# The first batch's attention and gates in two query parts (192 and 256 tokens) in a squared-ReLU attention and SwiGLU kernel

## The chip, the cores and the metric

The kernel runs on one core of one Trainium2 chip. The metric is the device time of one execution in microseconds (us). Engines: PE is TensorE (matmuls and transposes), DVE is VectorE, ACT is ScalarE, POOL is GpSimd, SP is SyncE. POOL and SP compute almost nothing here; their queues issue the DMAs.

## The reference

Eight batches, 12 heads, 448 tokens, 64 elements per head. The attention output of all heads becomes 3584 rows of 768; an RMS norm and a SwiGLU FFN follow.

```python
scores = matmul(q, k.T) / sqrt(64)               # per batch and head, 448 x 448
attn   = maximum(scores, 0) ** 2 / 448
x      = matmul(attn, v)                         # rows: batch, token; columns: head, element
xn     = x / sqrt(mean(x * x) + 1e-6) * rms_g
out    = (silu(xn @ w_gate) * (xn @ w_val)) @ w_out   # 768 -> 1536 -> 768, float32 out
```

## The kernel before, in words

**Units.** The work is written out as 24 attention units m: batch b = m // 3, and four heads (two pairs) in each. In a unit, `scores` (L272) makes seven tiles: for each pair three chunks of 128 keys, and one tile with the last 64 keys of both pairs. A tile holds two heads; its matmuls have 448 query columns and use half of PE's rows each. ACT takes the ReLU from PSUM (L297), DVE squares it in place (L298). `attend` (L301) multiplies with v a unit later, ACT scales the result into `xT` (L333) and DVE squares it into `x2` (L334). Keys stand in permuted order, and queries too: token = 7 x row + u, so a pair's queries are seven blocks u of 64.

**Norm and FFN.** After a batch's third unit, `norm` (L351) sums the squares with six constant-ones matmuls (psSS, L355), ACT takes the square root (L363), and DVE makes four reciprocals (L376) and six scaled tiles `xn` (L379). These DVE steps go into the list `bg` and are taken one by one by `step()`. Then `gates` (L398) puts 24 pieces into the list `pieces`, a gate piece (psG, L406, then Silu, L416) and a val piece (psV, L422, then the product hT, L429) for each of 12 blocks of 128 FFN columns, each six matmuls of 448 columns. After each second batch `outproj` (L443) adds 14 pieces of 12 matmuls (psO, L451); two halves of 384 columns are evacuated into one `ost` tile, by ACT (L467) and DVE (L469), and stored together by SP (L470).

**Order.** Nothing is scheduled by a tool: each engine runs in the order of the text. `fill(us)` (L479) takes pieces until their written costs (1.13 for a gate or val piece, 1.97 for a half of the out-projection) have used up the time given. Units up to the seventh get 6.8 us, later ones 13.8 (L500). While the first three units run there are no pieces; there, and in the first gate (L413), `warm` (L266) puts in matmuls of a constant tile whose result nobody reads (psW, L268).

**Buffers.** PSUM: two score tiles (psS) of two banks each, and four rotating banks (`rot`) for everything else, transposes too. `relu2` has nine r tiles, `ostage` two tiles, `sig` three.

**Loads and transposes.** POOL issues all loads of q, k, v and the weights in the order of the text (L144 to L170 first, the rest from `transposes` and `attend`); they convert float32 to bfloat16. q and k of batches 0 and 1, and q of batch 2, are turned on PE (psQ, psK, psX, L192) and copied by DVE (L210, L222, L258); later ones by DMA transposes on SP (`turn_by_dma`, L247), two per `fill`.

Of the kernel before, what the change touches and what calls it, by code (L numbers as in the profile page):

```python
# [15 lines left out]
def kernel(  # L16
# [33 lines left out]

    const_pool = ctx.enter_context(tc.tile_pool(name="consts", bufs=1))
# [6 lines left out]
    opool = ctx.enter_context(tc.tile_pool(name="ostage", bufs=2))  # L58
# [12 lines left out]
    nc.sync.dma_start(out=g_sb[:], in_=moe_rms_g.rearrange("(kt p) -> p kt", p=P))  # L71
# [20 lines left out]
    def load_q(pr, h0=0, h1=H, es=(0, 1)):  # L92
        for e in es:
            dst = q_t[pr][e * HALF : (e + 1) * HALF]
            src = q[2 * pr + e, h0:h1]
            if pr < 2:
                nc.gpsimd.dma_start(  # L97
                    out=dst[:, h0:h1],
                    in_=src.rearrange("h (p u) d -> p h u d", u=NU),
                )  # L100
            else:
                nc.gpsimd.dma_start(
                    out=dst, in_=src.rearrange("h (p u) d -> p u h d", u=NU)
                )

    def load_k(b, h0=0, h1=H):
        src = k[b, h0:h1, 0:XT0]
        if b < 2:
            nc.gpsimd.dma_start(
                out=k_t[b][:, h0:h1],  # L110
                in_=src.rearrange("h (p c) d -> p h c d", c=NCH),
            )
        else:
            nc.gpsimd.dma_start(
                out=k_t[b][:], in_=src.rearrange("h (p c) d -> p c h d", c=NCH)
            )

    def load_kx(b, h0=0, h1=H):
        nc.gpsimd.dma_start(
            out=kx_t[b][:, h0:h1], in_=k[b, h0:h1, XT0:S].rearrange("h p d -> p h d")  # L120
        )
# [22 lines left out]
    load_q(0, 0, 2, (0,))  # L144
# [3 lines left out]
    load_q(0, 2, 4, (0,))  # L148
    load_k(0, 2, 4)
    load_kx(0)  # L150
    load_v(0, 0, 4)
    eps_col = const_pool.tile([P, 1], FP32, name="eps_col", tag="eps_col")
    nc.vector.memset(eps_col[:], eps)  # L153
    load_q(0, 4, 8, (0,))
    load_k(0, 4, 8)
    load_vx(0)
    load_v(0, 4, 8)
    load_q(0, 8, 12, (0,))
    load_k(0, 8, 12)
    load_v(0, 8, 12)  # L160
    k_tile(1)
    load_q(0, 0, H, (1,))
    load_k(1)
    load_kx(1)
    load_gv(0, 256)
# [3 lines left out]
    load_gv(256, 512)  # L169
    load_gv(512, 768)  # L170
# [9 lines left out]
    QT, KTt, R, XT, X2 = {}, {}, {}, {}, {}  # L180
# [17 lines left out]
    def transposes(n):  # L198
# [4 lines left out]
        if pr == 0 or pr == 1 and e == 0:  # L203
            r0, r1 = (e * HALF, (e + 1) * HALF) if pr == 0 else (0, P)
            if j == 0 and e == 0:
                big(pr, None)
            ps = psum.tile([P, NU, r1 - r0], BF16, name="psQ", tag="rot", bufs=4)
            for u in range(NU):
                turn(ps[:, u, :], lambda hh: q_t[pr][:, 2 * j + hh, u, :], r0, r1)
            nc.vector.tensor_copy(out=QT[pr][:, j, :, r0:r1], in_=ps[:])  # L210
        if b < 2:
            if j == 0:
                big(None, b)
            ps = psum.tile([P, XT0], BF16, name="psK", tag="rot", bufs=4)
            for c in range(NCH):
                turn(
                    ps[:, c * P : (c + 1) * P],
                    lambda hh: k_t[b][:, 2 * j + hh, c, :],
                    0,
                    P,  # L220
                )
            nc.vector.tensor_copy(out=KTt[b][:, j, :XT0], in_=ps[:])  # L222
# [9 lines left out]
        if j == HP - 1:  # L232
            if b + 2 < B:
                k_tile(b + 2)
                load_k(b + 2)
                load_kx(b + 2)
            if e == 0 and pr + 1 < B // 2:
                q_tile(pr + 1)
                load_q(pr + 1)
            if b == 0:  # L240
                load_gv(768, 1024)
                load_gv(1024, F)
# [29 lines left out]
    def scores(m, slots, k=0):  # L272
        b, t = divmod(m, ND)
        qt, kt = QT[b // 2], KTt[b]
        for s in slots:
# [20 lines left out]
            r = rpool.tile([P, 2, S], BF16, name="r", tag="r")  # L296
            nc.scalar.activation(out=r[:], in_=ps[:, :, :S], func=ACT.Relu)  # L297
            nc.vector.tensor_tensor(out=r[:], in0=r[:], in1=r[:], op=ALU.mult)  # L298
            R[m, s] = r

    def attend(m):  # L301
# [26 lines left out]
        if t == 0:  # L328
            XT[b] = xpool.tile([P, KT, S], BF16, name="xT", tag="xT")
            X2[b] = xpool.tile([P, KT, S], BF16, name="x2", tag="x2", bufs=1)  # L330
        xt = XT[b][:, 2 * t : 2 * t + 2, :]
        for i in range(2):
            nc.scalar.mul(out=xt[:, i, :], in_=acc[i][:], mul=inv_attn)  # L333
        nc.vector.tensor_tensor(  # L334
            out=X2[b][:, 2 * t : 2 * t + 2, :], in0=xt, in1=xt, op=ALU.mult
        )
        if t == ND - 1 and b + 2 < B:
            v_tile(b + 2)
            load_v(b + 2)
            load_vx(b + 2)  # L340
            if b == 0:
                for f0 in range(0, FT, 4):
                    nc.gpsimd.dma_start(
                        out=wo_sb[:, f0 : f0 + 4], in_=wo_d[:, f0 : f0 + 4]
                    )
# [5 lines left out]
    def norm(b):  # L351
        ps = psum.tile([P, S], FP32, name="psSS", tag="rot", bufs=4)
        x2 = X2.pop(b)
        for kt in range(KT):
            nc.tensor.matmul(  # L355
                out=ps[:],
                lhsT=ones_bf[:, :P],
                rhs=x2[:, kt, :],
# [5 lines left out]
            out=rstd[:],  # L364
            in_=ps[:],
# [4 lines left out]
        xn = xpool.tile([P, KT, S], BF16, name="xn", tag="xn")  # L370
        xt = XT.pop(b)

        def recip(i):
            w = S // 4
            sl = slice(i * w, (i + 1) * w)
            nc.vector.reciprocal(out=rstd[:, sl], in_=rstd[:, sl])  # L376

        def scale(kt):
            nc.vector.scalar_tensor_tensor(  # L379
                out=xn[:, kt, :],  # L380
                in0=xt[:, kt, :],
                scalar=g_sb[:, kt : kt + 1],
                in1=rstd[:],
# [4 lines left out]
        for i in range(4):  # L388
            bg.append(lambda i=i: recip(i))
        for kt in range(KT):  # L390
            bg.append(lambda kt=kt: scale(kt))

        def ready():
            gates(b, xn)

        bg.append(ready)

    def gates(b, xn):  # L398
        pr, e = divmod(b, 2)

        def gate(fb, st):
# [3 lines left out]
            for kt in range(KT):  # L405
# [7 lines left out]
                if b == 0 and fb == 0 and kt < KT - 1:  # L413
                    warm(2)
            sig = tpool.tile([P, S], BF16, name="sig", tag="sig", bufs=3)
            nc.scalar.activation(out=sig[:], in_=ps[:], func=ACT.Silu)  # L416
            st["sig"] = sig

        def val(fb, st):
            ps = psum.tile([P, S], FP32, name="psV", tag="rot", bufs=4)  # L420
            for kt in range(KT):
# [9 lines left out]
                in0=st["sig"][:].rearrange("p (u x) -> p u x", u=NU),  # L431
# [11 lines left out]
    def outproj(pr):  # L443
        ob = out[2 * pr * S : 2 * (pr + 1) * S, :].rearrange("(x u) m -> x u m", u=NU)

        def half(u, o, st):
            if o == 0:
                st["ost"] = opool.tile([P, DM], FP32, name="ost", tag="ost")
# [9 lines left out]
            dst = st["ost"][:, o * OW : (o + 1) * OW]  # L458
            if 2 * pr + 2 == B and u == NU - 1:
                hw = OW // 2  # L460
                nc.scalar.copy(out=dst[:, :hw], in_=ps[:, :hw])
                nc.vector.tensor_copy(out=dst[:, hw:], in_=ps[:, hw:])
                lo = o * OW
                nc.scalar.dma_start(out=ob[:, u, lo : lo + hw], in_=dst[:, :hw])
                nc.sync.dma_start(out=ob[:, u, lo + hw : lo + OW], in_=dst[:, hw:])
            elif o == 0:
                nc.scalar.copy(out=dst, in_=ps[:])  # L467
            else:
                nc.vector.tensor_copy(out=dst, in_=ps[:])  # L469
                nc.sync.dma_start(out=ob[:, u, :], in_=st["ost"][:])  # L470

        for u in range(NU):
            st: dict = {}
            for o in range(2):
                pieces.append((1.97, lambda u=u, o=o, st=st: half(u, o, st)))
# [3 lines left out]
    def fill(us, idle_steps=3):  # L479
# [4 lines left out]
        while pieces and debt > 0:  # L484
# [3 lines left out]
            step()  # L488
# [5 lines left out]

    N = B * ND
    warm_tile()
    warm(8)
    transposes(0)
    for m in range(N + 1):
        rate = 6.8 if m < 2 * ND + 1 else 13.8  # L500
        first = m == ND
        idle = 2 if m <= ND else 0
        if m <= ND:
            warm_tile()
        if m < N:
            scores(m, (0, 1), idle if m == 0 else 0)
        if m == ND + 1:
            warm_tile()
            warm(3)
        if m in (ND + 1, 2 * ND + 1):  # L510
            fill(0.36 * rate)
        if m > 0:
            warm(idle // 2)
            attend(m - 1)
        else:
            transposes(1)
            last_keys(0)
        if m < N:
            scores(m, (2, 3), idle)
        if not first:  # L520
            fill(0.36 * rate)
        if 0 < m < N - 1:
# [3 lines left out]
            if m < ND:  # L526
                warm_tile()
        if m > 0 and m % ND == 0:
            norm(m // ND - 1)
        if m in (ND, 2 * ND):  # L530
            while bg:
                step()
        if first:
            warm_tile()
        if m < N:
            scores(m, (4, 5), idle)
        if m == 0:
            transposes(2)
        if not first:
            fill(0.36 * rate)  # L540
        if m < N:
            scores(m, (6,))
        if m + 1 < N:
            transposes(2 * m + 3)
            if m == 0:
                last_keys(1)
        if not first:
            fill(0.28 * rate)
# [32 lines left out]
```

## Time and profile before

| | us |
|---|---|
| median of three runs | 471.22 (470.94 to 472.3) |
| the profiled execution | 473.52 |
| its span, first to last instruction | 471.7 |
| PE busy in the span | 457.4 (97%) |
| DVE, ACT busy | 253.2, 253.9 (54% each) |
| constant matmuls psW: 60, busy on PE | 19.5 |

A row of the timeline has the start of a group of like instructions, its length, engine, line and operation, the tile written and those read, the count, and in brackets the idle time before it and who ended that. Rows of matmuls overlap, because they are pipelined; the distance between starts tells what a group costs. In the row of a group, "busy, mean ns" is followed by the idle time of the engine just before and by whoever ended it. The digits show 40 equal slices of the span in tenths of busy time.

### The profile page before, as it was taken

The page shows a single profiled execution, that of the slowest core. Times are in us where ns is not written, and L with a number is a line of the kernel's source. Part 1 is how long each engine was busy: PE and PEld are TensorE (multiplying, and loading weights), DVE is VectorE, ACT ScalarE, POOL GpSimd, SP SyncE. Part 2 cuts the span into 40 slices and gives each one's busy share as a digit, 9 for nine tenths or more (in the row PEclk, how much of TensorE's full clock was granted, in tenths as well). Part 3 has the DMA queues.
Part 4 walks back from the last instruction along what each step waited for, and adds up shares of the span by engine and source line. Part 5 has one row for each costly group of instructions (what it writes and reads, how often), then busy time and mean ns, then how long its engine had stood idle before and what let it go on. Part 6 is the DMA issues. An engine that isn't in the chain of part 4 may idle for free.

```text
span 471.7 us, 7484 instructions
## 1 busy us (share of the span) xinstructions
PE 457.4 (97%) x3048; PEld 223.9 (47%) x3048; DVE 253.2 (54%) x435; ACT 253.9 (54%) x366; POOL 68.8 (15%) x75
## 2 busy tenths in 40 slices
PE   8989998899999999989999999999999999999997
PEld 3344443444455544434455544444455544545564
DVE  2678665955436654675456545765456553732211
ACT  3788576655465375665565465765565274422110
POOL 8635113421040002500040002000000000000000
PEclk9999999999999999999999999999999999999999
DMA  9999999999989814990098618200002210000022
GB/s 93 175 185 183 175 173 152 192 144 120 47 103 176 215 44 74 161 101 0 2 125 168 158 52 114 14 1 1 1 0 101 82 53 1 0 1 1 35 100 101
DMA packets 129715, 42.77 MB, mean 91 GB/s; under 512 B 113424, under 2 KB 126224, under 8 KB 129680
## 3 DMA queue, kind: packets, MB, share of 16 engines
q0 software_dynamic: 96336, 24.38, 63.8%
q1 hardware_dynamic: 33056, 17.70, 18.1%
q8 instruction: 24, 0.39, 0.4%
q10 hardware_dynamic: 288, 0.20, 0.1%
q14 instruction: 11, 0.09, 0.1%
HBM read 48.76 MB, written 11.01 MB: 127 GB/s over the span
## 4 chain that ended last, share of the span: by engine, by line
PE 79%; DMA 14%; DVE 3%; ACT 2%; POOL 1%; issue 1%; DVEq 0%; POOLq 0%
PE psO L451 24%; PE psV L422 21%; PE psG L406 20%; DMA wv_sb<-in_moe_w_val_dram 9%; PE psS L289 6%; PE psAV L321 6%; DMA kld<-in_k_dram 5%; PE psSS L355 1%; ACT r L297 1%; DVE xn L379 1%; DVE rstd L376 1%; DVE hT L429 0%; DVE r L298 0%; POOL qld L97 0%; ACT xT L333 0%
## 5 line engine op out<-in xcount | busy, mean ns | idle before, releaser
L297 ACT ACTIVATE r<-psS 128x896 bf16<-128x896 f32 x168 | 145.9, 923 | 39.0 <-PE psS L289 39.0
L298 DVE TENSOR_TENSOR r<-r 128x896 bf16<-128x896 bf16 x168 | 104.0, 625 | 91.2 <-ACT r L297 90.7
L406 PE MATMUL psG<-xn,wg_sb 128*128 128x448 bf16 x576 | 125.9, 353 | 2.2 <-DVE hT L429 1.1
L422 PE MATMUL psV<-xn,wv_sb 128*128 128x448 bf16 x576 | 124.9, 353 | 1.7 <-DMA wv_sb<-in_moe_w_val_dram 1.5
L451 PE MATMUL psO<-wo_sb,hT 128*128 128x384 bf16 x672 | 113.0, 326 | 0.0
L416 ACT ACTIVATE sig<-psG 128x448 bf16<-128x448 f32 x96 | 52.2, 545 | 106.6 <-PE psG L406 91.4
L429 DVE TENSOR_TENSOR hT<-sig,psV 128x448 bf16<-128x448 bf16 x96 | 59.1, 617 | 61.8 <-PE psV L422 59.5
L451 PEld LDWEIGHTS <-hT 128*128 128x128 bf16 x672 | 64.3, 98 | 46.1 <-issue 4.8
L406 PEld LDWEIGHTS <-wg_sb 128*128 128x128 bf16 x576 | 55.1, 98 | 55.4 <-issue 5.6
L422 PEld LDWEIGHTS <-wv_sb 128*128 128x128 bf16 x576 | 54.1, 98 | 57.2 <-issue 7.9
L289 PE MATMUL psS<-QT,KT 64*128 64x448 bf16 (+1 forms) x384 | 53.1, 364 | 3.8 <-ACT r L297 3.8
L467 ACT COPY ost<-psO 128x384 f32<-128x384 f32 x27 | 12.9, 479 | 54.7 <-PE psO L451 47.9
L469 DVE COPY ost<-psO 128x384 f32<-128x384 f32 x27 | 15.0, 556 | 37.3 <-PE psO L451 37.3
L124 POOL DMA_DIRECT2D vld<-in_v_dram x10 | 9.5, 948 | 171.1 <-PE psAV L321 159.4
L289 PEld LDWEIGHTS <-KT 64*128 64x128 bf16 (+1 forms) x384 | 14.0, 96 | 40.6 <-issue 38.3
L321 PE MATMUL psAV<-r,vld 128*64 128x448 bf16 x288 | 31.8, 356 | 0.0
L379 DVE SCALAR_TENSOR_TENSOR xn<-xT,g_sb,rstd 128x448 bf16<-128x448 bf16 x48 | 30.8, 679 | 0.1
L333 ACT ACTIVATE xT<-psAV 128x448 bf16<-128x448 f32 x48 | 23.6, 544 | 6.1 <-PE psAV L321 5.9
L376 DVE RECIPROCAL rstd<-rstd 128x112 f32<-128x112 f32 x32 | 25.2, 824 | 2.9 <-ACT rstd L363 2.9
L334 DVE TENSOR_TENSOR x<-xT 128x896 bf16<-128x896 bf16 x24 | 15.0, 625 | 14.2 <-ACT xT L333 14.2
L321 PEld LDWEIGHTS <-vld 128*64 128x64 bf16 x288 | 14.4, 109 | 15.6 <-issue 7.6
L268 PE MATMUL psW<-ones_bf 128*128 128x448 bf16 x60 | 19.5, 421 | 1.4 <-DVE eps_col L153 1.4
(37 smaller groups left out, 160.5 us busy)
## 6 DMA issues: line engine op xcount, KB each, us to landing
out_dram<-ost SPq DMA_DIRECT2D x27, 384.0 KB, 2.3
qld<-in_q_dram POOLq DMA_DIRECT2D x7, 672.0 KB, 19.8
kld<-in_k_dram POOLq DMA_DIRECT2D x7, 576.0 KB, 15.1
vld<-in_v_dram POOLq DMA_DIRECT2D x7, 576.0 KB, 7.2
wo_sb<-in_moe_w_out_dram POOLq DMA_DIRECT2D x3, 768.0 KB, 23.9
vxld<-in_v_dram POOLq DMA_DIRECT2D x16, 96.0 KB, 7.7
wg_sb<-in_moe_w_gate_dram POOLq DMA_DIRECT2D x4, 384.0 KB, 14.6
wv_sb<-in_moe_w_val_dram POOLq DMA_DIRECT2D x4, 384.0 KB, 15.5
```

Source lines behind the costliest of these rows:

```text
L289: nc.tensor.matmul(out=ps[rows, hh, :S].rearrange("k (u x) -> k u x", u=NU), lhsT=kt[prt, j, keys], rhs=qt[prt, j, :, b % 2 * HALF : (b % ...
L297: nc.scalar.activation(out=r[:], in_=ps[:, :, :S], func=ACT.Relu)
L298: nc.vector.tensor_tensor(out=r[:], in0=r[:], in1=r[:], op=ALU.mult)
L321: nc.tensor.matmul(out=acc[i][hh * D : (hh + 1) * D, :], lhsT=w[rows, hh, :], rhs=r[rows, hh, :], start=(c == 0), stop=(c == NCH),)
L333: nc.scalar.mul(out=xt[:, i, :], in_=acc[i][:], mul=inv_attn)
L376: nc.vector.reciprocal(out=rstd[:, sl], in_=rstd[:, sl])
L379: nc.vector.scalar_tensor_tensor(out=xn[:, kt, :], in0=xt[:, kt, :], scalar=g_sb[:, kt : kt + 1], in1=rstd[:], op0=ALU.mult, op1=ALU.mult,)
L406: nc.tensor.matmul(out=ps[:], lhsT=wg_sb[:, kt, fb * P : (fb + 1) * P], rhs=xn[:, kt, :], start=(kt == 0), stop=(kt == KT - 1),)
L416: nc.scalar.activation(out=sig[:], in_=ps[:], func=ACT.Silu)
L422: nc.tensor.matmul(out=ps[:], lhsT=wv_sb[:, kt, fb * P : (fb + 1) * P], rhs=xn[:, kt, :], start=(kt == 0), stop=(kt == KT - 1),)
L429: nc.vector.tensor_tensor(out=HT[pr, fb][:, :, e * HALF : (e + 1) * HALF], in0=st["sig"][:].rearrange("p (u x) -> p u x", u=NU), in1=ps[:] ...
L451: nc.tensor.matmul(out=ps[:], lhsT=HT[pr, fk][:, u, :], rhs=wo_sb[:, fk, o * OW : (o + 1) * OW], start=(fk == 0), stop=(fk == FT - 1),)
```

## The change

The first batch's 448 queries are split into blocks u 0 to 2 (192 tokens) and u 3 to 6 (256 tokens). The kernel runs all three units of the first part, its norm and its first gates before it goes through the second part, whose units stand among the first part's gates. Score tiles of a part hold two chunks of keys (columns 2 x 192 or 2 x 256), r tiles grow to 1024 columns. Gate and val pieces of a part hold two FFN blocks. k and q of the first batch are turned two pairs at a time. The constant matmuls go from 60 to 42. Units 3 to 6 get 4.0 us of pieces, units 7 to 11 12.0, later ones 13.4. `fill` can take more than one DVE step behind a piece. The squares of a unit are written into `xn`, which the norm overwrites. Each half of the out-projection is stored by itself, from three half-wide `ost` tiles. Weights are loaded ahead of the second batch's k, q and v. The code:

```diff
+    US = ((0, 3), (3, NU))
...
-    opool = ctx.enter_context(tc.tile_pool(name="ostage", bufs=2))
+    opool = ctx.enter_context(tc.tile_pool(name="ostage", bufs=3))
...
+    def load_q0(h, h0=0, h1=H):
+        u0, u1 = US[h]
+        nc.gpsimd.dma_start(
+            out=q_t[0][:HALF, h0:h1, u0:u1],
+            in_=q[0, h0:h1].rearrange("h (p u) d -> p h u d", u=NU)[:, :, u0:u1],
+        )
...
-    load_q(0, 0, 2, (0,))
+    load_q0(0, 0, 2)
     load_k(0, 0, 2)
...
-    load_q(0, 2, 4, (0,))
     load_k(0, 2, 4)
+    load_q0(0, 2, 12)
+    load_k(0, 4, 8)
     load_kx(0)
     load_v(0, 0, 4)
+    load_vx(0)
+    load_k(0, 8, 12)
+    load_v(0, 4, 12)
...
+    load_q0(1)
+    load_gv(0, 256)
+    load_gv(256, 512)
+    load_gv(512, 768)
     k_tile(1)
-    load_q(0, 0, H, (1,))
     load_k(1)
     load_kx(1)
-    load_gv(0, 256)
+    load_q(0, (1,))
+    load_gv(768, 1024)
     v_tile(1)
     load_v(1)
     load_vx(1)
-    load_gv(256, 512)
-    load_gv(512, 768)
+    load_gv(1024, F)
...
+    PARTS = ((0, 1), (2, 3), (4, 5), (6,))
+    def part_scores(h, t, tiles, k=0, late=None):
+        u0, u1 = US[h]
+        w = (u1 - u0) * HALF
...
+            nc.scalar.activation(out=r, in_=ps[:, :, : n * w], func=ACT.Relu)
+            square(r, late)
...
+    def norm(b, parts, ready):
...
+        n = 4 if w > 256 else 2
...
+    def part_gates(h, fbs):
+        def both(w_sb, fb, name):
+            ps = psum.tile([P, 2, w], FP32, name=name, tag="rot", bufs=4)
+            for i in range(2):
+                for kt in range(KT):
+                    nc.tensor.matmul(out=ps[:, i, :],
+                        lhsT=w_sb[:, kt, (fb + i) * P : (fb + i + 1) * P],
+                        rhs=XN[0][:, kt, sl], start=(kt == 0), stop=(kt == KT - 1))
+                    if h == 0 and fb == 0 and i == 0 and w_sb is wg_sb and kt < KT - 1:
+                        warm(1)
...
+        cost = 12 * w / 2370
...
-            sig = tpool.tile([P, S], BF16, name="sig", tag="sig", bufs=3)
+            sig = tpool.tile([P, 512], BF16, name="sig", tag="sig")
...
-            step()
+            for _ in range(max(steps, round(cost))):
+                step()
...
+    big(0, 0)
+    first_q(0, 0, (0,))
+    first_k(0, (0,))
+    warm(1)
+    part_scores(0, 0, (0,), late=late)
+    warm(2)
+    first_q(0, 0, (1,))
+    first_k(0, (1,))
+    flush(late)
+    part_scores(0, 0, (1, 2))
+    last_keys(0)
+    first_k(1)
+    first_q(0, 1)
+    part_scores(0, 0, (3,))
+    warm_tile()
+    for t in range(1, ND):
+        part_scores(0, t, (0,))
+        warm(1)
+        part_scores(0, t, (1,))
+        part_attend(0, t - 1)
+        if t + 1 < ND:
+            first_k(t + 1)
+            first_q(0, t + 1)
+            warm_tile()
+        part_scores(0, t, (2, 3))
+    first_q(1, 0)
+    first_q(1, 1)
+    warm_tile()
+    warm(2)
+    part_attend(0, ND - 1)
+    warm(5)
+    norm(0, cols(0), lambda: part_gates(0, (0, 2, 4, 6)))
+    drain()
+    warm_tile()
+    part_scores(1, 0, (0, 1, 2, 3), 2)
+    warm(7)
+    warm_tile()
+    piece(2)
+    part_scores(1, 1, (0, 1))
+    part_attend(1, 0)
+    piece(1)
+    part_scores(1, 1, (2, 3))
+    first_q(1, 2)
+    piece(1)
+    part_scores(1, 2, (0, 1))
+    part_attend(1, 1)
+    piece(1)
+    part_scores(1, 2, (2, 3))
+    transposes(HP - 1)
+    transposes(HP)
+    last_keys(ND)
+    piece(1)
+    part_attend(1, 2)
+    prefetch_v(0, ND - 1)
+    transposes(HP + 1)
+    warm_tile()
+    warm(2)
+    norm(0, cols(1), lambda: part_gates(1, (0, 2, 4, 6)))
+    scores(ND, (0, 1), late=late)
+    piece(1)
+    steps(4)
+    piece(1)
+    scores(ND, (2, 3), late=late)
+    drain()
+    flush(late)
+    for h in range(2):
+        part_gates(h, (8, 10))
+    for m in range(ND, N + 1):
+        rate = 4.0 if m < 2 * ND + 1 else 12.0 if m < 4 * ND else 13.4
+        quick = 2 if m in (2 * ND, 2 * ND + 1) else 1
...
```

New helpers: `first_q` and `first_k` turn the first batch's q part and k for two pairs with one DVE copy each; `part_attend` is `attend` at a part's width; `square` squares an r tile at once or, given the list `late`, when `flush` is called; `piece(n)` runs n pieces, `drain()` all DVE steps. In the loop, a unit's three fills stand where they stood, the third unit's from after its second pair of score tiles on.

## The prediction

> **What bounds the kernel now.** I read the page's busy table and slices first, then the order of TensorE's (PE's) work by time, then who PE waits for.
>
> ```profile
> PE 457.4 (97%) x3048; PEld 223.9 (47%) x3048; DVE 253.2 (54%) x435; ACT 253.9 (54%) x366; POOL 68.8 (15%) x75
> ...
> DMA  9999999999989814990098618200002210000022
> ...
> PE 79%; DMA 14%; DVE 3%; ACT 2%; POOL 1%; issue 1%; DVEq 0%; POOLq 0%
> ...
> L268 PE MATMUL psW<-ones_bf 128*128 128x448 bf16 x60 | 19.5, 421 | 1.4 <-DVE eps_col L153 1.4
> ```
>
> PE is the bound, but 97% hides two things: 60 of its matmuls are the constant ones (psW, L268), and the DMA engines are full for the first 130 us, so a load lands when the bytes ahead of it are through.
>
> ```profile
> 12.28 0.93 PE L268 MATMUL psW<-ones_bf 128*128 128x448 bf16 x2
> 13.14 0.49 PE L289 MATMUL psS<-QT,KT 64*128 64x448 bf16 x2
> 13.56 0.55 PE L268 MATMUL psW<-ones_bf 128*128 128x448 bf16 x2
> ...
> 44.22 0.35 PE L406 MATMUL psG<-xn,wg_sb 128*128 128x448 bf16 x1 [0.23 <-DVE xn L379]
> ...
> 72.92 1.31 PE L422 MATMUL psV<-xn,wv_sb 128*128 128x448 bf16 x6 [1.53 <-DMA wv_sb<-in_moe_w_val_dram]
> ...
> 91.36 1.29 PE L406 MATMUL psG<-xn,wg_sb 128*128 128x448 bf16 x6 [1.11 <-DVE hT L429]
> ...
> 204.41 0.36 PE L289 MATMUL psS<-QT,KT 64*128 64x448 bf16 x2 [1.39 <-ACT r L297]
> 205.22 0.36 PE L289 MATMUL psS<-QT,KT 64*128 64x448 bf16 x2 [0.45 <-ACT r L297]
> ```
>
> The first three rows are the clock: the same pair of constant matmuls takes 0.93 at 12.3 us and 0.55 at 13.6, so PE ran at half clock up to about 13.4 us. The fourth is the first gate matmul, at 44.2 us: until then there is no FFN work. The rest are the later stalls.
>
> So I book the span as useful PE work plus lost time. Unit costs, start to start: gate or val group of six, 1.14 us (0.189 each at 448 columns); out-projection, 1.95 for twelve (0.1625 at 384). The two rows give 0.414 ns a column, so 0.083 at 192 and 0.110 at 256. A group that follows another tiling of the array takes about 0.10 more (gate groups show 1.24 against 1.14). Scores 1.75 a unit, attention 1.57. Over the instruction list: gates and vals 1152 x 0.189 = 217.9, out-projection 109.2, 24 units of scores and attention 42.0 + 37.7, norm sums 9.1, transposes 11.5 (0.34 and 0.51 for q, 0.29 for k), some 60 returns from tiled work at 0.10; together 433.6 us of useful work. The profiled span is 471.7: 34.5 are lost up to the last matmul's start and 3.5 follow it. At 44.2 us, 20.4 are done and 23.9 lost; when 32.7 are done, 27.0 are lost (ten more constants are in the first gate); 7.5 come later: 1.6 (wv_sb), 1.5 (first norm beside units, 88 to 91 us), 2.2 (202 to 205 us: six score tiles in a row, the FFN list being empty), the rest small.
>
> **The change, part by part.**
>
> Work added to PE. First batch's scores: a 192-wide tile of two chunks is 2 x 0.083 + 0.105, so a unit 3 x 0.271 + 0.21 = 1.02, a 256-wide one 1.21, together 2.23 for 1.75. Attention 0.83 + 1.02 for 1.57. Three units: 3 x (0.48 + 0.28) = 2.3. Gates and vals: 144 times 0.083 + 0.110 - 0.189, 0.5. Sum +2.8. Not shown by any row is whether a 128-column weight load keeps up with 83 ns; weight loads show 98 ns each, but the 128-row q transposes pass 14 loads of 64 columns with their matmuls in 0.51 us, so 128 loaded columns in 73 ns. Bounds: 0 and 144 x (98 - 83) = 2.2. I take 0: of the two rows this one shows a rate, the other a latency that overlaps.
>
> Constants: 60 become 42, of which 18 x 0.189 = 3.4 less at full clock; this is inside the lost time below.
>
> The opening. ACT rows, start to start: 0.81 for a 896-wide relu (five in 4.15), 0.44 for 448; so 0.70 at 768, 0.39 at 384, 0.92 at 1024, 0.23 and 0.28 for the evacuations. DVE: square 0.53 at 896, so 0.47 and 0.60; reciprocal 0.72 at 112; scale 0.60 at 448, between 0.26 and 0.60 at 192: I take 0.34. With these I went down the built order of the three engines:
> - POOL's queue: heads 2 to 12 of the first q part (240 KB) go in one load ahead of k's heads 4 to 8, of kx and of v. By bytes moved in this trace (567 KB by 8 us, 1123 by 12, 2020 by 17, landings 1 to 2.5 us later) they land at 8.9, kx at 11.9, the first v at 12.9, last v at 18.6, second q part at 22, first gate weights at 24 to 26, the sixth at 34.5, all gate and val weights by 52 instead of 81. The second unit's scores then start at 14.5, after the k and q copies.
> - A 192-wide unit needs 2.95 on ACT and some 3 on DVE, but at half clock 5.1 on PE (1.65 scores, 1.4 attention, 1.65 transposes, a constant): PE bounds it. Third unit at 20.2, last attention to 26.9, norm sum to 29, sqrt 0.4, two reciprocals 1.3, scales to 32.5, four score tiles of the second part beside it on ACT (3.2), seven constants: first gate at 33.8, if the clock is half until about 30 us. If it is full from 20 us, 30.7; from 13.4 us, 27.7.
> When does the clock rise? In before PE streamed 80, 71 and 77% of full-array work in the three 3.4 us stretches up to 13.4 us. By the same count the new order has 34, 41, 70, 42, 76, 67% in the stretches from 6.6 to 27 us, and 95% only after that. I take late.
>
> [...]
>
> So 10.6 us of useful work are done at 33.8: 23.2 lost, 0.7 less than before at its first gate, and five constants in that gate for ten.
>
> Second part's attention among the gates (33.8 to 62.6). Useful 22.1 us, constants 1.4. Waits found by going down the queues: 1.0 for the q copy, which stands behind two squares on DVE; 0.6 at the third attention; 0.8 and 1.8 in the second norm, where the PSUM buffer of a val piece waits for a q copy that stands behind four scales and four put-off squares; rest 1.1. Elapsed 28.8, so at 32.7 useful us 29.9 are lost: 2.9 more than before. ACT has two more table loads here (1.28 each).
>
> Later. Weights have landed, so 1.6 goes; next late would be the third batch's k, whose load now stands behind the weights on POOL: it lands at about 60 and its transposes on SP run to 84, each chunk needed from 82 on, in order; cover about 10 us for the first chunks, 5 for that batch's q (72 against 77). The empty list at 202 us goes: the new rates leave at least 11 us of FFN in each unit from the eighth on. Units four to six with little FFN: 10.3 and 8.3 us on PE against 7.4 on ACT and about 7 on DVE, so PE still bounds and I find 0.2. The second batch's norm: DVE has 14 us of work in a stretch of 12.6, a val waits 0.5 and an attention 1.0; 1.5 as before. Small stalls stay (1.9). Sum 3.6 for 7.5.
>
> At nothing: the norm gain's load, later in the text but still first on SP's queue; the scaled activations that now overwrite their squares, since they wait for the norm sum anyway; half stores (each copy still waits for the store three pieces back; 2.3 us landing under 7 us of PE work; 27 more issues of 0.33 us on SP; cost if cover fails, the 1.3 us ACT already waits for ost). Two sig buffers for three: a gate waits for the product two pieces, over 2 us, back; bounds 0 and 0.6 (a product) in each of the norms. The last stores are split as before.
>
> Sum on the span: useful +2.8; lost 29.9 + 3.6 = 33.5 for 34.5, -1.0. Span 473.5, +1.8. The profiled execution took 473.5 with 471.7 of span, 2.3 over the median of 471.2; the same 1.8 on the median is **473.0**.
>
> **Rivals.**
> - The clock rises early (by 13 to 20 us). First gate 27.7 to 30.7, 3.1 to 6.1 sooner, and nothing behind it changes: 466.9 to 469.9, faster. It decides if the clock is full before about 20 us. For: PE is nearly always occupied, and the row does not tell whether the chip counts occupation or fill. Against: the fill shares above.
> - It comes out even: clock at 24 to 27 us, first gate near 32, what the opening gives is spent on smaller pieces and the second norm. 470 to 472.5.
> - Weight loads bound the 192-wide pieces (98 ns for 83): +2.2, 475.2, and up to 476.5 with the norms' sig waits.
>
> **How the numbers follow.** Measurement of this kernel can tell about 0.3% (1.4 us: 469.8, 472.6). Forecast, 471.8 to 474.5: 0.42 (slower 0.34, same 0.08). Early clock: 0.32 (faster 0.30, same 0.02). Even: 0.15 (same 0.13, faster 0.02). Weight loads: 0.11, slower. So faster 0.32, same 0.23, slower 0.45. The range leaves out the earliest clock's tail and half of the last case: 467.2 to 476.0.
>
> **What would show it.** Constant matmuls of 0.37 us start to start after 20 us: the clock step right; 0.19 at 14 us: wrong. First psG at 33.8. val pieces (psV) waiting for QT copies at about 60 us. Gate matmuls of the first batch at 83 and 110 ns. No wait for wv_sb, no score tiles waiting for ACT at about 200 us; none for KT at 80 to 90 us. The forecast is wrong if the first gate comes before 31 us or the stretch behind it takes under 26 us.

## The result, and the profile after

The changed kernel takes **473.87 us** (median of eleven runs, 473.18 to 475.79). The kernel before, run beside it, takes 471.22 (468.87 to 473.34). The ratio is 1.0061, interval 1.0038 to 1.0084: slower by about 0.6%. The profiled execution, the slowest of the eleven, took 475.79 with a span of 474.0, against 473.52 and 471.7 before. Executions more than 1.5% above the fastest of their kernel are left out of all ratios.

From the page of the changed kernel: PE's busy time, the granted clock in 40 slices, and the shares of the chain that ended last.

```profile
PE 459.7 (97%) x3276; PEld 240.7 (51%) x3276; DVE 254.1 (54%) x455; ACT 256.6 (54%) x378; POOL 67.8 (14%) x73
...
PEclk8579899999999999999999999999999999999999
...
PE 81%; DMA 6%; ACT 5%; DVE 5%; issue 2%; SPq 1%; POOL 1%; ACTq 0%; POOLq 0%
```

PE is as full as before, and busy for 2.3 us longer. New is the clock row: 8 and 5 in the first two slices, 7 in the third, 8 in the fifth (47 to 59 us). The trace records full clock from 4.89 to 8.30 us, half to 28.79, full to 56.09, half to 59.51, and full from there on.

PE's timeline of the changed kernel, the rows that answer to those of before:

```profile
6.23 0.55 PE L303 MATMUL psW<-ones_bf 128*128 128x448 bf16 x2
8.77 0.37 PE L190 MATMUL psQ<-ident,qld 64*64 64x64 bf16 x6 [1.98 <-DMA qld<-in_q_dram]
...
23.66 0.93 PE L303 MATMUL psW<-ones_bf 128*128 128x448 bf16 x2
...
29.56 0.55 PE L303 MATMUL psW<-ones_bf 128*128 128x448 bf16 x2
...
33.23 0.25 PE L530 MATMUL psG<-xn,wg_sb 128*128 128x192 bf16 x1
...
41.93 0.61 PE L372 MATMUL psS<-QT,KT 64*128 64x256 bf16 x8 [1.06 <-DVE QT L255]
...
47.57 0.84 PE L408 MATMUL psAV<-r,vld 128*64 128x256 bf16 x12 [0.58 <-DVE QT L210]
...
50.73 1.16 PE L530 MATMUL psG<-xn,wg_sb 128*128 128x192 bf16 x12
51.73 1.15 PE L530 MATMUL psV<-xn,wv_sb 128*128 128x192 bf16 x12
...
54.60 0.25 PE L190 MATMUL psX<-ident,kxld 64*64 64x64 bf16 x4 [0.60 <-ACT sig L548]
55.41 0.37 PE L335 MATMUL psS<-QT,KT 64*128 64x448 bf16 x2 [0.56 <-ACT r L344]
56.22 0.56 PE L335 MATMUL psS<-QT,KT 64*128 64x448 bf16 x2 [0.44 <-ACT r L344]
56.71 2.74 PE L530 MATMUL psG<-xn,wg_sb 128*128 128x256 bf16 x12
60.19 1.47 PE L530 MATMUL psV<-xn,wv_sb 128*128 128x256 bf16 x12 [0.73 <-ACT sig L548]
...
65.34 1.48 PE L530 MATMUL psG<-xn,wg_sb 128*128 128x256 bf16 x12
66.66 1.47 PE L530 MATMUL psV<-xn,wv_sb 128*128 128x256 bf16 x12
```

The pair of constants tells the clock: 0.55 at 6.2 us, 0.93 at 23.7, 0.55 again at 29.6. Between the first two stands a wait of 1.98 us for the second pair's q. The first gate comes at 33.23. In the second part's norm PE waits 0.60, 0.56, 0.44 and 0.73 us for ACT; between them twelve gate matmuls take 2.74 us at 56.7, at half clock (1.48 at 65.3).

Booked as in the prediction (useful work and lost time, lost time taken at the start of a PE group; constants, waits and half clock are lost time). Useful work has the prediction's costs and lost time is what is left of the elapsed time, so each row adds up by construction:

| profiled run of | half clock | first gate | useful, lost there | lost at 32.7 useful | lost to last start | span |
|---|---|---|---|---|---|---|
| before | to 13.4 | 44.2 | 20.4, 23.9 | 26.9 | 34.5 | 471.7 |
| after | 8.3–28.8, 56.1–59.5 | 33.2 | 10.6, 22.6 | 29.7 | 34.1 | 474.0 |

The opening gains 1.3, the stretch behind it loses 4.1 (7.1 for 3.0), the rest gains 3.2 (4.4 for 7.6), and useful work costs 2.8.

### The profile page after: what moved, and what is told of

Read it like the earlier page. It is cut to its first block, busy times and chain, and to the rows that moved or that the text cites. A ratio compares the mean times of both kernels' runs of the same rounds, so it can differ in the third digit from the quotient of the medians.

```text
span 474.0 us, 8047 instructions
## 1 busy us (share of the span) xinstructions
PE 459.7 (97%) x3276; PEld 240.7 (51%) x3276; DVE 254.1 (54%) x455; ACT 256.6 (54%) x378; POOL 67.8 (14%) x73
## 4 chain that ended last, share of the span: by engine, by line
PE 81%; DMA 6%; ACT 5%; DVE 5%; issue 2%; SPq 1%; POOL 1%; ACTq 0%; POOLq 0%
PE psO L617 21%; PE psG L575 20%; PE psV L589 20%; PE psS L335 6%; PE psAV L437 5%; DMA KT<-kld 4%; PE psW L303 2%; ACT r L344 2%; PE psSS L484 1%; PE psAV L408 1%; DVE r L311 1%; PE psS L372 1%; DMA out_dram<-ost 1%; ACT r L383 1%; DVE xn L506 1%
## 5 line engine op out<-in xcount | busy, mean ns | idle before, releaser
L311 DVE TENSOR_TENSOR r<-r 128x896 bf16<-128x896 bf16 (+4 forms) x171 | 103.9, 615 | 96.1 <-ACT r L344 87.5
L344 ACT ACTIVATE r<-psS 128x896 bf16<-128x896 f32 x147 | 128.0, 924 | 24.3 <-PE psS L335 24.2
L575 PE MATMUL psG<-xn,wg_sb 128*128 128x448 bf16 x504 | 109.4, 353 | 0.2 <-DVE xn L506 0.2
L589 PE MATMUL psV<-xn,wv_sb 128*128 128x448 bf16 x504 | 109.2, 353 | 0.0
L633 ACT COPY ost<-psO 128x384 f32<-128x384 f32 x28 | 13.4, 479 | 67.6 <-PE psO L617 50.4
L506 DVE SCALAR_TENSOR_TENSOR xn<-xT,g_sb,rstd 128x448 bf16<-128x448 bf16 (+2 forms) x54 | 31.5, 628 | 0.3
L454 ACT ACTIVATE xT<-psAV 128x448 bf16<-128x448 f32 (+2 forms) x54 | 24.3, 503 | 10.3 <-PE psAV L408 5.4
L503 DVE RECIPROCAL rstd<-rstd 128x112 f32<-128x112 f32 (+2 forms) x32 | 25.0, 822 | 4.4 <-ACT rstd L492 4.4
L383 ACT ACTIVATE r<-psS 128x768 bf16<-128x768 f32 (+3 forms) x24 | 18.8, 830 | 13.7 <-PE psS L372 13.5
L455 DVE TENSOR_TENSOR xn<-xT 128x896 bf16<-128x896 bf16 (+2 forms) x27 | 15.5, 573 | 11.3 <-ACT xT L454 11.3
L115 POOL DMA_DIRECT2D kld<-in_k_dram x11 | 16.5, 1496 | 24.3 <-DMA KT<-kld 20.7
```

The lines of the kernel that those rows point to most:

```text
L311: nc.vector.tensor_tensor(out=r, in0=r, in1=r, op=ALU.mult)
L344: nc.scalar.activation(out=r, in_=ps[:, :, :S], func=ACT.Relu)
L454: nc.scalar.mul(out=xt[:, i, sl], in_=acc, mul=inv_attn)
L503: nc.vector.reciprocal(out=rstd[:, cs], in_=rstd[:, cs])
L506: nc.vector.scalar_tensor_tensor(out=xn[:, kt, sl], in0=xt[:, kt, sl], scalar=g_sb[:, kt : kt + 1], in1=rstd[:, :w], op0=ALU.mult, op1=ALU ...
L575: nc.tensor.matmul(out=ps[:], lhsT=wg_sb[:, kt, fb * P : (fb + 1) * P], rhs=xn[:, kt, :], start=(kt == 0), stop=(kt == KT - 1),)
```

## The experiments

Each was timed beside the kernel before; ratios are to that. "Half clock" comes from the trace's records of the granted clock; before the first record the length of the constants tells it (a pair takes 0.93 us at half clock and 0.55 at full, as above).

**1. a_qsplit.** Is the opening slow because the second pair's q comes in one large load?

```diff
+    load_q0(0, 2, 4)
     load_k(0, 2, 4)
-    load_q0(0, 2, 12)
+    load_q0(0, 4, 12)
```

> The changed kernel with the 240 KB load of q heads 2 to 12 cut in two again: heads 2 to 4 (48 KB) ahead of k heads 2 to 4, heads 4 to 12 behind them. Theory A (the opening is held at half clock, and PE's 2.0 us wait for this load is what drops the clock at 8.3 us): second psQ at about 7 us instead of 8.8, no clock drop in the opening or a much shorter one, first gate at 28 to 31 us instead of 33.2, 2 to 4 us less in all, ratio to before 0.998 to 1.002. Theory B (the opening is set by the chain through ACT and DVE and by the loads, the clock is beside the point; the change is slower because of 2.8 us more PE work): first gate at 32 to 33, under 1 us less in all, ratio 1.004 to 1.007.

Ratio 1.0102 (1.0062 to 1.0142), 475.96 us; spans 470.8 to 474.9, against 471.4 to 474.0 of the changed kernel. PE's timeline of a_qsplit:

```profile
7.33 0.37 PE L191 MATMUL psQ<-ident,qld 64*64 64x64 bf16 x6
...
11.34 0.32 PE L191 MATMUL psX<-ident,kxld 64*64 64x64 bf16 x4 [2.06 <-DMA kxld<-in_k_dram]
```

The wait for q is gone and a wait of 2.06 for kx stands behind it; the clock is at half until 26.9 us and the first gate comes at 32.5. The wait moved, the time did not fall.

**2. a_warm.** Do the missing constants cost the clock?

```diff
     part_scores(0, 0, (0,), late=late)
-    warm(2)
+    warm(8)
...
     for t in range(1, ND):
+        warm(2)
         part_scores(0, t, (0,))
-        warm(1)
+        warm(2)
```

> The changed kernel with six more constant matmuls in front of the second psQ and three more in each of the next two units: 12 more in all, put where PE waits. Theory A: they hold the clock at full through the opening in most executions, first gate at 28 to 31 us, 1.5 to 4 us less in all. Theory B: PE only works more; first gate at 33 to 35, 0 to 1.5 us more in all.

Ratio 1.0032 (1.0006 to 1.0058), 471.99 us. Half clock 11.8 to 22.0 (10.2 us for 20.5), first gate 31.9. PE's timeline of a_warm has a new wait behind it:

```profile
82.62 0.55 PE L335 MATMUL psS<-QT,KT 64*128 64x448 bf16 x4 [1.82 <-DMA KT<-kld]
```

PE comes earlier, the third batch's KT does not; the wait is followed by 3.4 us of half clock. (This execution has a span of 473.2; of the eleven others ten have 468.0 to 470.6, and a recorded clock above its 0.985, so the wait need not be in them.)

**3. b_rates.** The later rates alone, in the kernel before.

```diff
-        rate = 6.8 if m < 2 * ND + 1 else 13.8
+        rate = 6.8 if m < 2 * ND + 1 else 12.0 if m < 4 * ND else 13.4
```

> The kernel before with one part of the change alone: from the eighth unit on 12.0 us of pieces a unit up to the twelfth, 13.4 later, in place of 13.8. Theory A: the empty list at 202 us and its 2.2 us stall go, nothing else changes: 1.8 to 2.2 us less, ratio 0.995 to 0.997. Rival (the stall only moves to another unit, or the tail takes it back): ratio 0.999 to 1.001.

Ratio **0.9934** (0.9912 to 0.9956), 467.27 us: the fastest of all, faster than both kernels. The clock is full from 4.3 us to the end, the first gate (opening unchanged) comes at 41.35 for 44.22, and the starvation at 202 us is gone. PE's timeline of b_rates:

```profile
41.35 0.35 PE L406 MATMUL psG<-xn,wg_sb 128*128 128x448 bf16 x1 [0.22 <-DVE xn L379]
```

So the code that opens the kernel before can be 2.9 us sooner than in its profile; what differs between the two is the clock.

**4. b_stores.** Half stores alone, in the kernel before.

```diff
-    opool = ctx.enter_context(tc.tile_pool(name="ostage", bufs=2))
+    opool = ctx.enter_context(tc.tile_pool(name="ostage", bufs=3))
...
+            ost = opool.tile([P, OW], FP32, name="ost", tag="ost")
...
+            nc.sync.dma_start(out=ob[:, u, lo : lo + OW], in_=ost[:])
```

> The kernel before with one part of the change alone: each half of the out-projection stored by itself from three half-wide ost tiles. Theory A: costs and saves nothing, ratio 0.999 to 1.001. Rival (27 more issues on SP put the DMA transposes late, or ost tiles come free later and hold ACT and DVE): 0.5 to 1.5 us more.

Ratio 0.9995 (0.997 to 1.002). Half stores cost nothing that can be seen. Its trace also shows what the empty list at 200 us does besides starving PE. PE's timeline of b_stores:

```profile
199.97 0.36 PE L289 MATMUL psS<-QT,KT 64*128 64x448 bf16 x2 [1.39 <-ACT r L297]
200.78 0.50 PE L289 MATMUL psS<-QT,KT 64*128 64x448 bf16 x2 [0.45 <-ACT r L297]
201.21 2.42 PE L406 MATMUL psG<-xn,wg_sb 128*128 128x448 bf16 x6
203.42 1.73 PE L422 MATMUL psV<-xn,wv_sb 128*128 128x448 bf16 x6
```

Six gate matmuls take 2.42 us for 1.30: the clock is at half from 200.88 to 204.3. Waits of 1.8 us cost 1.8 and then some 1.5 more (203.42 - 201.21 is 2.21 for 1.14, 204.99 - 203.42 is 1.57 for 1.14). The kernel before seems to meet this in about half of its executions. Beside a_fill, nine of seventeen have a recorded clock of 0.995 or 0.996, as the execution of b_stores shown here, and spans of 468.9 to 469.8; the other eight have 0.999 or more and, but for one, 467.2 to 467.9. No trace of it shows the drop itself.

**5. a_kt.** Third batch's k and q ahead of the last weights, as in the kernel before.

```diff
-    load_gv(1024, F)
...
+            if b == 0:
+                load_gv(1024, F)
```

> The changed kernel with the last third of the gate and val weights (1.5 MB of the 4.7 MB) loaded behind the third batch's k and q again, as before the change. In the profile with the twelve more constants PE waited 1.8 us for the third batch's KT, and 0.25 in the profile of the change, where the opening and the halved clock at 56 us had already made PE late. Theory A (behind the late opening stands the DMA order: KT comes at 82 to 84 us whatever the opening does): KT some 6 us earlier, no wait for it, 0.3 to 1.8 us less, ratio 1.002 to 1.006. Rival (KT just happens to come in time, the order of loads is beside the point): no difference to the change, ratio 1.005 to 1.008; a wait for weights at 70 to 75 us would make it slower.

Ratio 1.009 (1.0062 to 1.0117), 474.88 us. No wait for KT at 80 to 90 us, and no gain: by itself the order of the weights is not what costs.

**6. a_order.** One gate piece moved ahead of the second norm's sum (L735 for L740).

```diff
+    piece(1)
     warm_tile()
     warm(2)
     norm(0, cols(1), lambda: part_gates(1, (0, 2, 4, 6)))
     scores(ND, (0, 1), late=late)
-    piece(1)
     steps(4)
     piece(1)
```

> The changed kernel with one gate piece of the first part put ahead of the second norm's sum instead of behind the first score tiles. ACT then takes its Silu before the table of the square root is loaded, so that the four waits for ACT at 54 to 60 us (2.3 us in the profile) shrink and with them the idle share that halves the clock for 3.4 us at 56 us in some executions. Theory A (this stretch is held by ACT's table loads and order, not by PE's work): those waits 1 us or less, no clock drop there, 1 to 3 us less, ratio 0.999 to 1.004. Rival (the norm, 1 us later, only moves the waits to the scaled activations): 0 to 1 us more.

Ratio 1.0095 (1.0067 to 1.0123), 475.79 us. The 0.60 for ACT's sigmoid goes, 0.61 for a ReLU of ACT stands at 52.0 us, and the val piece waits longer. PE's timeline of a_order:

```profile
58.56 1.47 PE L530 MATMUL psV<-xn,wv_sb 128*128 128x256 bf16 x12 [1.52 <-DVE QT L210]
```

The stall moves by one place. (The profiled run, at a span of 480.5, also held a wait of 6.9 us for KT, for which the other runs' spans of 471.5 to 475.3 leave no room; nothing is concluded from it.)

**7. a_all.** Experiments 2, 5 and 6 together.

> The changed kernel with all three: twelve more constants in the opening, the last third of the weights behind k and q, the gate piece ahead of the norm. Theory A: the gains add, since each takes away the next wait: 468 to 470 us, ratio 0.997 to 1.001. Theory B (2.8 us of more PE work bound it): no better than the twelve constants alone, 1.003.

Ratio 1.0051 (1.0034 to 1.0068), 473.45 us. Half clock 11.5 to 21.8; no wait for KT; the 1.52 of a_order is there again. The hoped-for 468 to 470 did not come.

**8. b_rates4.** All three rates of the change, in the kernel before.

```diff
-        rate = 6.8 if m < 2 * ND + 1 else 13.8
+        rate = 4.0 if m < 2 * ND + 1 else 12.0 if m < 4 * ND else 13.4
```

> The kernel before with all three new rates: 4.0 us of pieces in the first units too, then 12.0 and 13.4. The later rates alone gave 0.9934. Theory A (units with 4.0 us of pieces are still bound by PE, 8.6 us against 8.0 on ACT and DVE): as the later rates alone, 0.993 to 0.996. Rival (with so little FFN work PE waits for the ReLUs, and the waits halve the clock): 1 to 4 us more than the later rates alone.

Ratio 0.997 (0.9942 to 0.9998), 468.98 us. With less FFN work beside units 3 to 6, PE reaches the third batch sooner than its KT. PE's timeline of b_rates4:

```profile
70.17 0.55 PE L289 MATMUL psS<-QT,KT 64*128 64x448 bf16 x4 [2.04 <-DMA KT<-kld]
```

Set beside b_rates, the low early rate gives back about half of what the later rates bring.

**9. b_cold.** Does the kernel before need its constants? 16 of 60 left out of its first three units.

```diff
-        idle = 2 if m <= ND else 0
+        idle = 1 if m < ND else 2 if m == ND else 0
```

> The kernel before with 16 of the 60 constant matmuls left out of its first three units (44 stay); nothing else is touched. Theory A (the constants hold the clock in the opening): the granted clock is at half for longer in the first 30 us than in the kernel before (whose profile has it at half to 13.4 us, and whose fastest runs, with a span of 467.2, must have it at full nearly from the start), the first gate comes 1 to 5 us later than the 41.4 to 44.2 us seen so far, and the time is 1.003 to 1.010 of before. Theory B (in the opening PE waits for ACT's ReLUs anyway, and the constants only fill those waits): the first gate comes within 0.5 us of 41.4 to 44.2, and the ratio is 0.997 to 1.001.

Ratio 0.9997 (0.998 to 1.0014). Theory A failed in its sizes: in the profile the clock was full from 4.3 us, with one stretch at half (28.2 to 31.6), and the first gate came at 40.99. Its clock did fall more often: the twelve executions have a recorded clock of 0.985 to 0.996, those of the kernel before beside them 0.995 to 1.0. The time is the same, so what the constants cost and what they hold are about even.

**10. a_hot.** 22 more constants in the changed kernel, and the load order of a_kt.

```diff
     part_scores(0, 0, (0,), late=late)
-    warm(2)
+    warm(14)
...
     for t in range(1, ND):
+        warm(3)
         part_scores(0, t, (0,))
-        warm(1)
+        warm(3)
```

> The changed kernel with 22 constant matmuls more in the first part's units (64, about as many as before the change; 12 of them in the wait for the second pair's q at 8 us), and with the last gate and val weights loaded behind the third batch's k and q. Theory A (too few constants let the clock fall in the opening): the clock is at half for at most 7 us of the first 30, where the changed kernel had 20.5 us, the first gate comes at 29 to 31 us for 33.2, no wait for KT near 82 us, and the time is 468.5 to 470.5, ratio 0.997 to 1.001. Theory B (behind the clock stands the chain of ReLUs, squares and norm on ACT and DVE, and added constants only take its place): first gate at 31.5 us or later, ratio 1.002 to 1.006.

Ratio 1.0053 (1.0032 to 1.0074), 472.52 us. The opening did what theory A said: one stretch at half clock (12.0 to 15.4), first gate at 30.32. The time did not; the one execution with a recorded clock of 1.0 is the fastest, 469.64 us. PE's timeline of a_hot:

```profile
11.44 0.25 PE L189 MATMUL psX<-ident,kxld 64*64 64x64 bf16 x4 [1.16 <-DMA kxld<-in_k_dram]
...
53.80 2.70 PE L531 MATMUL psG<-xn,wg_sb 128*128 128x256 bf16 x12
```

Half clock still follows the wait of 1.16 in the opening, and again the waits of the second norm (12 gate matmuls in 2.70).

**11. a_rate68.** The changed kernel with the early rate of before.

```diff
-        rate = 4.0 if m < 2 * ND + 1 else 12.0 if m < 4 * ND else 13.4
+        rate = 6.8 if m < 2 * ND + 1 else 12.0 if m < 4 * ND else 13.4
```

> The changed kernel with 6.8 us of FFN pieces for 4.0 in units 3 to 6. In the kernel before, 4.0 for 6.8 cost about 1.7 us. Theory A (the low early rate is what makes the changed kernel slow): ratio to before 1.000 to 1.003, 471.5 to 472.5 us, no wait for KT at 83 us. Theory B (the first batch's pieces are partly used up among its second part, and the low rate saves what is left): the list is empty in the sixth unit, PE waits 2 to 4 us there for ReLUs and transposes, and the ratio is 1.006 to 1.012.

Ratio 1.0249 (1.0222 to 1.0275), 481.72 us. Theory B's place was right, its price too low. PE's timeline of a_rate68:

```profile
97.51 0.38 PE L437 MATMUL psAV<-r,vxld 64*64 64x448 bf16 x4 [0.90 <-DVE r L311]
...
99.77 0.36 PE L335 MATMUL psS<-QT,KT 64*128 64x448 bf16 x2 [0.84 <-ACT r L344]
...
105.17 0.53 PE L575 MATMUL psG<-xn,wg_sb 128*128 128x448 bf16 x1 [1.85 <-DVE xn L506]
105.50 2.44 PE L589 MATMUL psV<-xn,wv_sb 128*128 128x448 bf16 x6
```

The first batch's pieces are spent before the second batch's gates exist: a row of waits, then half clock. The low early rate is a consequence of the split, not a fault beside it.

**12. a_fill.** In the traces so far half clock stood behind waits and small tiles, where PE has little array work (shares in the last section). The rule of the expectation is the author's estimate from them: array work put into such a stretch keeps the clock at full. This kernel is a_hot with 14 constants more, put in the waits ahead of the two drops.

```diff
     part_scores(0, 0, (1, 2))
+    warm_tile()
+    warm(7)
     last_keys(0)
...
             transposes(2 * m + 2)
+            if m == ND:
+                warm_tile()
+                warm(3)
             if m + 1 < 2 * ND:
                 last_keys(m + 1)
...
-            scores(m, (4, 5))
+            scores(m, (4, 5), 2 if m == ND else 0)
```

> The kernel of a_hot with 14 constant matmuls more (78): 7 in the wait for kx at 10 us, 7 in the waits for ACT at 51 to 55 us. [...] By the rule the clock is full from 2 to 6 us on to the end, in the profile and (span 467.5 to 468.5) in most runs, the first gate comes at 29.0 to 30.0 us, and the time is 469.3 to 470.3, ratio 0.998 to 1.002. Rival (the waits come from ACT and DVE, and constants in them push real work back, or the drops have another cause): a half window remains between 8 and 16 us or between 50 and 60 us in the profile, and the ratio stays at 1.003 to 1.007. [...]

Ratio **1.0004** (0.9989 to 1.002), 470.5 us, with 36 constants more than the changed kernel. From the page of a_fill, the clock row:

```profile
PEclk9999999999999999999999999999999999999999
```

From PE's timeline of a_fill, the first gate and the second norm:

```profile
29.98 0.25 PE L531 MATMUL psG<-xn,wg_sb 128*128 128x192 bf16 x1
...
51.35 0.73 PE L304 MATMUL psW<-ones_bf 128*128 128x448 bf16 x3 [0.60 <-ACT sig L549]
...
53.75 1.48 PE L531 MATMUL psG<-xn,wg_sb 128*128 128x256 bf16 x12
...
55.97 1.47 PE L531 MATMUL psV<-xn,wv_sb 128*128 128x256 bf16 x12 [0.73 <-ACT sig L549]
```

The waits for ACT are still there; the gate matmuls take 1.48 for 2.74. Full clock from 7.4 us to the end in the profile, a recorded mean clock (which leaves out the start) of 0.999 or more in all twelve runs, first gate at 29.98. With constants in the waits ahead of them, neither drop came. The ratio is inside the range expected. The median is 0.2 us above its range, and eight of the twelve spans (468.6 to 470.7) lie above the 467.5 to 468.5 expected; in the profile the clock rose at 7.4 us and not at 2 to 6.

## Why the prediction was right, point by point

The forecast, 473.0, is 0.9 us from the 473.87 measured; on its own execution it said 473.5 of span for 474.0. Slower was called with 0.45.

- **Useful work +2.8: about 0.9 too high.** 192-wide groups of twelve stand 1.00 us apart (50.73 to 51.73, 83 ns each), 256-wide ones 1.32 (65.34 to 66.66, 110): weight loads bound nothing, and that rival is out. Attention took 1.01 (36.80 to 37.81) and, at full clock in a_fill, 0.83 (15.71 to 16.54), as booked. The scores were mis-sized: a 256-wide unit's took about 1.0 us (0.54 from 36.26 to 36.80, 0.46 from 38.90 to 39.36) for 1.21, a 192-wide one's 0.92 in a_fill (0.27, 0.27 and 0.38 from 18.84, 19.79 and 20.88 on) for 1.02. Over three units that is 0.9, so the rows give about 1.9; the rest stands as lost time in the table above.
- **First gate at 33.8, 23.2 lost: 33.2 and 22.6.** The clock step went by the share of the array that is filled and came near: half until 28.8, forecast until about 30. It was wrong about the start: the clock rose at 4.9 us and fell at 8.3 behind the q wait, which the step had not seen (it had q landing at 8.9, but took no wait from it). How near the hit is, is partly luck. Three more profiled executions run the same opening on PE; they are at half until 23.1 to 23.8 us and have the first gate at 31.0 (a_rate68), 31.8 (a_order) and 32.1 (a_kt). That is close to what the rival that comes out even had for the opening (clock at 24 to 27 us, first gate near 32), and the 31.0 is just under the forecast's own sign of being wrong.
- **29.9 lost at 32.7 useful: 29.7.** The 1.0 for the q copy (1.06) and 0.6 at the third attention (0.58) stood where they were said to. **The second norm was mis-sized:** the "0.8 + val 1.8" was 1.6 ahead of the gate piece and 0.73 at the val piece, which waited for ACT's sigmoid and not for a q copy; in place of the difference came 1.4 for half clock (2.75 for 1.32 from the gate piece's start to the end of PE's work on it), a cost that no step had.
- **3.6 lost later: 4.4.** No wait for wv_sb, none at 200 us, as forecast. **The cover of KT failed:** about 10 us were claimed, and the first chunk waited 0.25 us at 83.8 in the changed kernel and 1.82 in a_warm, whose opening is 1.3 us faster. It cost next to nothing here, and a_warm suggests that this is because the opening was slow.
- **Half stores at nothing: held** (0.9995). Sig buffers, two for three, were not tried alone; the waits named "ACT sig" come while ACT has two table loads of 1.28 us and ReLUs ahead of the sigmoid.
- **The early-clock rival was priced too well.** It had "nothing behind it changes". With the clock full almost throughout (a_hot and a_fill, with 22 and 36 constants more) the first gate comes at 30.3 and 30.0, not 27.7, and the time is 472.5 and 470.5, not 466.9 to 469.9.

**Where the expected gain went.** By ratios, which multiply (each is known to 0.002 or 0.003): the three rates without the split, 0.9970; the split with the clock held, 1.0004 / 0.9970 = 1.0034, about +1.6 us (a_fill also has a_kt's load order, which alone showed no gain); the clock, 1.0061 / 1.0004 = 1.0057, about +2.7 us. The first is a gain that needs no split, and with the old early rate it is 0.9934. The second is a lower bound: six of b_rates4's twelve executions have a recorded clock of only 0.993 to 0.996, as have, at 0.995 or 0.996, nine of the seventeen of the kernel before beside a_fill. The eight others of these take 469.3 us in the median; with the clock held on both sides the split is some 1.2 us slower than the kernel before (470.5), the rates included.

The split by itself buys little for a plain reason: the first gate moves from 41.35 us (b_rates) to 29.98 (a_fill), 11.4 us, but with 10.6 us of useful work done for 20.4. Lost time at the first gate is 19.4 for 21.0; at 32.7 useful us it is 25.5 for 24.0. The second part's stretch among the gates eats the 1.6 and 1.5 more, and useful work is longer: 2.8 in the prediction's costs, with which these lost times are booked, about 1.9 by the rows. What each wait in that stretch costs by itself was not measured; a_order shows only that one of them moves when pushed.

## What to carry to other kernels

Book useful work against lost time at the same point of the work, not at the same landmark: a first gate 11 us sooner was worth 1.6 us. When work is cut into smaller pieces, look in the trace for half clock behind waits and small tiles. There a short wait was paid for twice (waits of 1.8 us and then some 1.5 more in b_stores), and constants put into the waits themselves were cheap (14 in a_fill, at a ratio of 1.0004 for the 1.0053 of a_hot). Undo a change in parts even when it loses: the one line of rates in it was worth 0.7%.

## What the runs showed of the hardware that was not expected

**Half clock came behind stretches with little array work.** I divided the changed kernel's opening, and the part ahead of its later drop, at the records of the clock and into pieces of 3.41 us between them, and added up each piece's array work: columns of a matmul, times the rows and columns of the array that it uses, as a share of what full clock could do. A column is counted at 0.416 ns, half of what the constants show at half clock (448 columns start 0.373 us apart). Where in its record a matmul is counted moves a share by up to 0.05.

| piece from | clock | share | next |
|---|---|---|---|
| 1.5 | half | 0.44 | full |
| 4.9 | full | 0.26 | half |
| 8.3, 11.7, 15.1, 18.5 | half | 0.21, 0.29, 0.32, 0.32 | half |
| 22.0 | half | 0.365 | half |
| 25.4 | half | 0.46 | full |
| 52.7 | full | 0.26 | half |

By the same count a_hot has 0.25 and 0.33 ahead of its two drops; in a_fill, with constants there, neither came. b_rates has shares of 0.41 to 0.77 from 4.3 to 41.8 us and full clock all through; the changed kernel loses full clock at 8.3 us and does not get it back for 20 us. PE's busy time does not tell the two apart: in the changed kernel PE is busy all through the pieces from 15.1 and 22.0 us (3.41 us in each), and the clock stays at half. What in the chip sets the clock the traces do not show.

The clock's cost here, ramp and later drops, is 0.6% (1.0061 for 1.0004), as much as the whole verdict.

**The clock row leaves out the start.** Before the first record the page counts full clock: the kernel before shows a row of nines though a pair of its constants takes 0.93 us up to 12.3 us and 0.55 from 13.6 on. The length of a matmul of known size tells the clock where the row does not.
